# Two Q/K buffers instead of three, and one more weight tile loaded beside attention

## The chip, the cores and the metric

The kernel runs on one core of a Trainium2 chip. The metric is device time in microseconds (us) of one execution; lower is better. The kernel before took 382.33 us (median of 3 runs, 381.64 to 383.32).

## The reference

A batch of 8 sequences of 448 tokens goes through 12 heads of attention with a sigmoid in place of the softmax. Its output, 3584 rows of 768, goes through a "soft" mixture of 8 experts: each expert sees 4 slots, a slot is a weighted mean over all rows, and every row takes back a weighted mean of the 32 slot results.

```python
# attention, per head: q, k, v are (448, 64)
scores = q @ k.T / sqrt(64) - log(448)
attn_out = sigmoid(scores) @ v
# mixture of experts on x (3584 x 768), phi (768 x 32)
logits = x @ phi
d = softmax of logits over the rows            # which rows go into a slot
slot_input = d.T @ x                           # 32 x 768
slot_out[e] = relu(slot_input[e] @ w1[e]) @ w2[e]   # w1[e] 768x1024, w2[e] 1024x768
c = softmax of logits over the slots
out = c @ slot_out                             # 3584 x 768
```

All is float32. The weights w1 and w2 are 25.2 MB each, 50.3 MB together: they are more than the core's on-chip memory holds, and they can be used only when the slot inputs are known, so after the attention of all 8 batches.

## The kernel before

**Attention.** The 96 heads are worked in 48 pairs. One Q/K tile (`qk`, 128 partitions x 896 floats, 3584 bytes a partition) holds the transposed Q and K of both heads of a pair. The 448 keys of a pair are cut into chunks of 128 with a rest of 64, and the rests of two neighbouring pairs are put together. So two pairs make seven steps: an even pair p has chunks 0, 1, 2 and a fourth step that does the rests of p and of p+1 together (so it reads both Q/K tiles), then the odd pair p+1 has chunks 0, 1, 2. There are 24 x 7 = 168 steps. Step i of the loop at L409 issues `score` (L161, TensorE: eight matmuls into PSUM, then the sigmoid on ScalarE at L165), and then `weigh` of the step two earlier (L190, TensorE: the product with V). On TensorE the two alternate, and everything else (row sums into x, transposes of x into y for the slot products, the logits and slot sums of the batch just finished) is placed between them on the other engines, or as short groups of matmuls at the batch borders (L230, L284).

**Loads.** Every DMA of the kernel is issued by SyncE (SP), in program order; an issue that has to wait holds up all that stand behind it. In the loop, step i issues, behind the `score`:

- `load_qk` (L140) where the step was the last that reads a pair's Q/K tile: the fourth step of an even pair (`u[1] == NFK`) and the last chunk of an odd pair. It fetches the pair three further on into the buffer that this step lets go, so it waits for the step's score matmuls;
- `load_unit` (L94) as often as the pace asks: a weight unit is 128 x 768 floats (3072 bytes a partition, 384 KB), 64 units make up w1 and 64 w2. `N_A` = 56 units are to be issued by step 140;

and, behind the `weigh`, `load_vl` (L152, the V rows of the rests) or `load_v` (L146), each waiting for the weigh matmuls that last read its buffer.

**On-chip memory.** The weight ring has `N_A + N_B` = 70 tiles. The first 56 (`wa`) have memory of their own. The other 14 (`wb`) are laid over the tiles of attention, in the order in which these were allocated (`first`, L112): qk0, qk1, v0, vl, att0, qk2, x0, att1, att2, v1, x1, and then y. In bytes a partition: qk and att 3584 each, v 1536, vl 512, x 5376, y 12288. A `wb` load (L465 and L466 issue all of them, behind everything that attention issues) waits until the last reader of each attention tile under it is done. From the 71st unit on a load goes into the ring's first tile again, when the expert matmuls (L472) have read it, and so on round the ring.

**After attention.** The eight experts' first products (L472, which use units 0 to 63), their second products (L579, units 64 to 127, in two halves of the columns), and the output rows (L536, L537), which SP writes in 28 stores of 384 KB (L543, L550) through ring tiles. The last units come in the second half of the second products, and 19 of the 28 stores follow the last of these products.

Of the kernel before, what the change touches and what calls it, by code (L numbers as in the profile page):

```python
# [19 lines left out]
NFK = 3  # L20
# [3 lines left out]
W_STEPS = 140  # L24
# [2 lines left out]
NFC = F // P  # L27
HALF = DM // 2
UNIT = 768
N_A = 56  # L30
N_B = 14
QW = 2 * S
NP = B * NPR
WARM = 8
# [14 lines left out]
def soft_moe_attention(ctx: ExitStack, tc: tile.TileContext, qk, v, vl, phi, w1, w2, cst, out):  # L49
# [26 lines left out]
    state = {"next": 0, "ring": 0, "wpb": None}  # L76
    utile = {}

    def ring_tile(dt=F32):
        n = state["ring"]  # L80
        state["ring"] = n + 1
        n %= N_A + N_B
        if n < N_A:
            return wpa.tile([P, UNIT], dt, name=f"wa{n}")
        return state["wpb"].tile([P, UNIT], dt, name=f"wb{n - N_A}")

    def load_unit():
        n = state["next"]
        if n >= len(units):
            return  # L90
        state["next"] = n + 1
        u = units[n]
        t = ring_tile()[:]
        nc.sync.dma_start(t, w1[u[1:]] if u[0] == "w1" else w2[u[1:]])  # L94
        utile[u] = t
# [4 lines left out]
    with ExitStack() as actx:  # L100
# [8 lines left out]
        def hold(kind, n=""):  # L109
            return ap.tile(kinds[kind], F32, name=f"{kind}{n}")  # L110

        first = [("qk", 0), ("qk", 1), ("v", 0), ("vl", ""), ("att", 0), ("qk", 2), ("x", 0)]  # L112
        first += [("att", 1), ("att", 2), ("v", 1), ("x", 1)]
        held = {k: hold(*k) for k in first}
        xs = [held.pop(("x", t)) for t in range(2)]
# [3 lines left out]
        def get(*k):  # L119
            return held.pop(k, None) or hold(*k)  # L120
# [15 lines left out]

        def load_qk(p):
            if p < NP:
                t = get("qk", p % 3)
                nc.sync.dma_start(t[:], qk[p])  # L140
                qkts[p] = t

        def load_v(p):
            if p < NP:
                t = get("v", p % 2)
                nc.sync.dma_start(t[:], v[p])  # L146
                vts[p] = t

        def load_vl(r):
            if 2 * r < NP:  # L150
                t = get("vl", "")
                nc.sync.dma_start(t[:], vl[r])  # L152
                vls[r] = t

        def score(u):
            p, c = u
            sc = ps_sc.tile([P, 2, 512], F32, name="sc")
            for t in range(2):
                pt, k0 = (p, c * P + t * 64) if c < NFK else (p + t, NFK * P)
                for h, r in enumerate(heads):  # L160
                    nc.tensor.matmul(  # L161
                        sc[64 * t:64 * t + 64, h, 0:S], qkts[pt][r, S + k0:S + k0 + 64], qkts[pt][r, 0:S],
                        start=True, stop=True)
            att = get("att", seq.index(u) % 3)
            nc.scalar.activation(att[:], sc[:, :, 0:S], AF.Sigmoid, bias=nbias[:], scale=QSCALE)  # L165
            atts[u] = att

        def weigh(u):
            p, c = u
            att = atts.pop(u)  # L170
            if c == 0 and p % 2 == 0:
                avs[p] = [ps_av.tile([P, 512], F32, name=f"av0{t}") for t in range(2)]
            if c == NFK:
                avs[p + 1] = [ps_av.tile([P, 512], F32, name=f"av1{t}") for t in range(2)]
            if p == NP - 1:
                for h, r in enumerate(heads):
                    nc.tensor.matmul(  # L177
                        avs[p][1][r, 0:S], vts[p][:, c, r], att[:, h, :], start=False, stop=(c == NFK - 1))
                return
            for t in range(2):  # L180
                row = slice(64 * t, 64 * t + 64)
                for h, r in enumerate(heads):
                    if c < NFK:
                        o, w = avs[p], vts[p][row, c, r]
                        start = c == 0 and (p % 2 == 0 or t == 0)
                        stop = c == NFK - 1 and (p % 2 == 1 or t == 1)
                    else:
                        o, w = avs[p + t], vls[p // 2][row, r]
                        start, stop = t == 1, t == 0
                    nc.tensor.matmul(o[t][r, 0:S], w, att[row, h, :], start=start, stop=stop)  # L190

        def evac_a(p):
            nc.scalar.copy(x_of(p), avs[p][1][:, 0:S])  # L193

        def evac_b(p):
            av = avs.pop(p)
            nc.vector.tensor_tensor(out=x_of(p), in0=x_of(p), in1=av[0][:, 0:S], op=ALU.add)  # L197
# [20 lines left out]
        def turn_pe(px, p):  # L218
            for c in range(NBK):
                n = P if c < NBK - 1 else 64  # L220
                nc.tensor.transpose(out=px[0:n, c * P:(c + 1) * P], in_=x_of(p)[:, c * P:c * P + n], identity=ident)
# [5 lines left out]
        def logits(lg, b, pairs, js=(3, 2, 1, 0)):  # L227
            for hp in pairs:
                for j in js:
                    nc.tensor.matmul(  # L230
                        lg[32 * j:32 * j + 32, 0:BLK * nblk(j)], phi_sb[:, hp, :],
                        blocks(x_of(b * NPR + hp), j, nblk(j)),
                        start=(hp == 0), stop=(hp == NPR - 1))
# [84 lines left out]
        def last_job(b, lgt, pw, px):  # L318
# [45 lines left out]
            return sT, finish  # L364

        load_qk(0)
        load_v(0)
        load_qk(1)
        load_vl(0)
        load_v(1)  # L370
        nc.sync.dma_start(phi_sb, phi)
        nc.sync.dma_start(csb[:], cst)
        load_qk(2)
        pw = ps_av.tile([P, 512], F32, name="av00")
        for _ in range(WARM):
            nc.tensor.matmul(pw[:, 0:WN], acc[:, 0:P], acc[:, 0:WN], start=True, stop=True)  # L376
# [4 lines left out]
        for r in range(NP // 2):  # L381
            p = 2 * r
# [3 lines left out]
        for b in range(B):  # L386
            u = b * per_b + LAG
# [4 lines left out]
        for b in range(B - 1):  # L392
            u = (b + 1) * per_b + LAG
# [9 lines left out]
        def work(n):  # L403
            while todo and n > 0:
                k, turn = todo.popleft()
                turn()
                n -= k

        for i in range(len(seq) + LAG):  # L409
            for f in early.get(i, ()):  # L410
                f()
            if i < len(seq):
                u = seq[i]
                score(u)
                if u[1] == NFK:
                    load_qk(u[0] + 3)
                elif u[0] % 2 == 1 and u[1] == NFK - 1:
                    load_qk(u[0] + 3)
                while state["next"] < min(N_A, (i + 1) * N_A // W_STEPS):
                    load_unit()  # L420
            if i == len(seq) - 1:
                lgt = ps_sc.tile([P, 2, 512], F32, name="sc")
                nc.vector.memset(lgt[64:128, 0, 96:128], NEG)
            if i == len(seq):
                dmx = small.tile([1, 1], F32, name="dmx")
                nc.scalar.activation(dmx[:], atts[seq[-1]][0:1, 0, 0:1], AF.Exp)
                logits(lgt[:, 0, :], B - 1, range(NPR - 1))
            for f in middle.get(i, ()):
                f()
            if i >= LAG:  # L430
                u = seq[i - LAG]
                weigh(u)
                p, c = u
                if c == NFK:
                    evac_b(p)
                    load_vl(p // 2 + 1)
                elif c == NFK - 1:
                    load_v(p + 2)
                    if p == NP - 1:
                        work(B * S)  # L440
                        pw = ps_av.tile([P, 512], F32, name="av00")
                        px = [ps_av.tile([P, 512], F32, name="av01")]
                        px += [ps_sc.tile([P, 2, 512], F32, name="sc")[:, 0, :], ps_av.tile([P, 512], F32, name="av10")]
                        turn_pe(px[0], p - 1)
                        continue
                    evac_a(p)
                    if p % 2 == 1:
                        evac_b(p)
            for f in late.get(i, ()):
                f()  # L450
            work(rate.get(i, PACE))
# [12 lines left out]

    for _ in range(N_B):  # L465
        load_unit()  # L466
# [184 lines left out]
```

## Time and profile before

| | |
|---|---|
| median of 3 runs | 382.33 us |
| the profiled execution | 382.41 us, of which the span from first to last instruction is 380.6 us |
| TensorE matmul busy | 357.8 us (94%) |
| VectorE / ScalarE busy | 252.7 us (66%) / 224.3 us (59%) |
| moved by DMA | 95.26 MB, mean 250 GB/s |
| weight units | 112 into `wa` tiles, 16 into `wb` tiles, 384 KB each |
| Q/K loads | 48 of 448 KB, median 3.5 us from issue to landing |

Busy shares are over the whole span, which here has two stretches with different limits; the page's rows of 40 slices (9.5 us each) show where one ends and the other begins. In the timeline a group of instructions has its start, its length and its count; "SPq" is SyncE's queue, whose rows are the issues of DMAs. "Landing" is the time from such an issue to the DMA's completion.

### The profile page before, as it was taken

Reading aid. Unit: us, or ns where it says so; the run is one execution under the profiler, and the core shown is the slowest. Engines: PE = TensorE matmul, PEld = TensorE weight load, DVE = VectorE, ACT = ScalarE, POOL = GpSimd, SP = SyncE. Lnnn points to the kernel's source line nnn. Section 1 sums busy time; section 2 is a strip of 40 time slices with the busy share of each in tenths; the row PEclk is TensorE's granted clock in tenths of the full one; section 3 lists DMA queues with packets and bytes.
Section 4 is the critical chain, followed back from the end, with each engine's and each line's share of the span. In section 5 each row is a group of like instructions: output and inputs, shape, how many; then the busy total and the mean of one; then the engine's idle time right before and its main releaser. Section 6 shows DMA issues by size and latency. Waiting matters only on the chain.

```text
span 380.6 us, 10176 instructions
## 1 busy us (share of the span) xinstructions
PE 357.8 (94%) x4132; PEld 158.4 (42%) x4132; DVE 252.7 (66%) x681; ACT 224.3 (59%) x310; POOL 4.9 (1%) x23
## 2 busy tenths in 40 slices
PE   8999999999999999999999999999999969989750
PEld 5444444444444444444444444444446533422430
DVE  0148868886889688788968896886846762132560
ACT  4777766766768677667767676776761213422450
POOL 0000000000000000000000000000000000100000
PEclk9999999999999999999999999999999987999895
DMA  7677575766656675757667575534369999999998
GB/s 258 212 252 255 165 257 176 254 217 189 219 190 216 235 241 197 236 180 246 213 186 250 169 236 203 146 102 134 91 219 388 397 397 400 397 400 395 396 399 301
DMA packets 42382, 95.26 MB, mean 250 GB/s; under 512 B 4448, under 2 KB 18528, under 8 KB 42336
## 3 DMA queue, kind: packets, MB, share of 16 engines
q1 hardware_dynamic: 42336, 94.62, 72.0%
q8 instruction: 32, 0.52, 0.5%
q14 instruction: 14, 0.11, 0.1%
HBM read 83.59 MB, written 11.01 MB: 249 GB/s over the span
## 4 chain that ended last, share of the span: by engine, by line
PE 83%; DVE 7%; DMA 3%; ACT 2%; issue 1%; DVEq 0%; ACTq 0%
PE sc L161 34%; PE av L190 33%; PE po L579 5%; PE sc L230 3%; PE sc L284 3%; DMA wb<-in_w_dram 2%; PE pt L517 2%; PE av L376 1%; PE ph L536 1%; DVE tmp L486 1%; DMA out_dram<-wa 1%; DVE tmp L485 1%; DVE wa L537 1%; PE pt L536 1%; PE av L177 1%
## 5 line engine op out<-in xcount | busy, mean ns | idle before, releaser
L165 ACT ACTIVATE att<-sc,nbias 128x896 f32<-128x896 f32 x168 | 169.2, 1008 | 85.2 <-PE sc L161 82.1
L161 PE MATMUL sc<-qk 64*64 64x448 f32 x1344 | 157.2, 538 | 0.4 <-ACT att L165 0.4
L212 DVE STREAM_TRANSPOSE y<-x 32x384 f32<-32x384 f32 (+5 forms) x352 | 143.4, 407 | 5.7
L190 PE MATMUL av<-att,v 64*64 64x448 f32 x1128 | 131.4, 536 | 0.0
L161 PEld LDWEIGHTS sc<-qk 64*64 64x64 f32 x1344 | 49.8, 133 | 72.6 <-issue 60.8
L190 PEld LDWEIGHTS av<-att,v 64*64 64x64 f32 x1128 | 43.1, 133 | 62.8 <-issue 61.3
L197 DVE TENSOR_TENSOR x<-x,av 128x448 f32<-128x448 f32 x47 | 29.2, 621 | 41.4 <-PE av L190 29.7
L579 PE MATMUL po<-wa,hw 128*32 128x384 f32 x224 | 24.8, 513 | 0.3 <-DMA wa<-in_w_dram 0.3
L193 ACT COPY x<-av 128x448 f32<-128x448 f32 x47 | 24.6, 523 | 0.0
L190 PE MATMUL av<-att,vl 64*64 64x448 f32 x192 | 22.4, 536 | 0.0
L472 PE MATMUL ph<-wa,phit 128*32 128x256 f32 x336 | 18.5, 379 | 0.0
L472 PEld LDWEIGHTS ph<-wa,phit 128*32 128x32 f32 x336 | 10.7, 110 | 6.9
L536 PE MATMUL ph<-lt,wb 128*128 128x384 f32 x28 | 12.7, 453 | 1.0 <-DVE lt L566 1.0
L537 DVE COPY wa<-pt 128x384 f32<-128x384 f32 x21 | 10.9, 554 | 2.9 <-PE pt L536 2.6
L537 ACT COPY wa<-ph 128x384 f32<-128x384 f32 x21 | 9.8, 480 | 4.9 <-PE ph L536 4.2
L230 PE MATMUL sc<-x,phit 128*32 128x96 f32 (+1 forms) x384 | 12.3, 262 | 0.3 <-DVE x L202 0.3
L230 PEld LDWEIGHTS sc<-x,phit 128*32 128x32 f32 x384 | 9.9, 110 | 6.2 <-ACT x L193 4.9
L536 PE MATMUL pt<-lt,wb 128*128 128x384 f32 x28 | 10.4, 373 | 1.6 <-DVE lt L566 1.6
L190 PEld LDWEIGHTS av<-att,vl 64*64 64x64 f32 x192 | 7.3, 133 | 10.7 <-issue 10.7
L306 DVE SCALAR_TENSOR_TENSOR acc<-acc,t,sc 128x192 f32<-128x192 f32 x6 | 2.5, 413 | 13.5 <-PE sc L284 13.5
L488 ACT COPY t<-tmp 128x32 f32<-128x32 f32 x8 | 1.7, 218 | 15.8 <-DVE tmp L486 15.8
L507 DVE CAST tmp<-lt 128x128 fp32r<-128x128 f32 x8 | 1.8, 227 | 13.7 <-PE pt L517 13.4
(106 smaller groups left out, 178.6 us busy)
## 6 DMA issues: line engine op xcount, KB each, us to landing
wa<-in_w_dram SPq DMA_DIRECT2D x112, 384.0 KB, 6.2
qk<-in_qk_dram SPq DMA_DIRECT2D x48, 448.0 KB, 3.5
v<-in_v_dram SPq DMA_DIRECT2D x48, 192.0 KB, 2.6
out_dram<-wa SPq DMA_DIRECT2D x21, 384.0 KB, 5.2
wb<-in_w_dram SPq DMA_DIRECT2D x16, 384.0 KB, 6.1
out_dram<-wb SPq DMA_DIRECT2D x7, 384.0 KB, 7.7
vl<-in_vl_dram SPq DMA_DIRECT2D x24, 64.0 KB, 2.6
csb<-in_cst_dram SPq DMA_DIRECT2D x1, 128.0 KB, 4.6
```

The lines of the kernel that those rows point to most:

```text
L161: nc.tensor.matmul(sc[64 * t:64 * t + 64, h, 0:S], qkts[pt][r, S + k0:S + k0 + 64], qkts[pt][r, 0:S], start=True, stop=True)
L165: nc.scalar.activation(att[:], sc[:, :, 0:S], AF.Sigmoid, bias=nbias[:], scale=QSCALE)
L190: nc.tensor.matmul(o[t][r, 0:S], w, att[row, h, :], start=start, stop=stop)
L193: nc.scalar.copy(x_of(p), avs[p][1][:, 0:S])
L197: nc.vector.tensor_tensor(out=x_of(p), in0=x_of(p), in1=av[0][:, 0:S], op=ALU.add)
L212: nc.vector.transpose(ys[t][32 * g:32 * g + 32, a, k0:k0 + n, 0:nblk(g), :], src)
L230: nc.tensor.matmul(lg[32 * j:32 * j + 32, 0:BLK * nblk(j)], phi_sb[:, hp, :], blocks(x_of(b * NPR + hp), j, nblk(j)), start=(hp == 0), sto ...
L284: nc.tensor.matmul(sl[32 * a:32 * a + 32, 0:SLN], zt[:, c * BLK:(c + 1) * BLK], yt[:, :, a, :, c, :], start=(c == 0), stop=(c == NBK - 1))
L472: nc.tensor.matmul(ph[32 * j:32 * j + 32, 0:256], sT[:, kc, :], utile[("w1", e, j, kc // 3)][:, kc % 3 * 256:(kc % 3 + 1) * 256], start=(k ...
L536: nc.tensor.matmul(pf[:, 0:HALF], ct_of(m), st, start=True, stop=True)
L537: (nc.scalar.copy, nc.vector.tensor_copy)[n % 2](ov, pf[:, 0:HALF])
L579: nc.tensor.matmul(po[32 * fl:32 * fl + 32, 0:HALF], h[:, k:k + NSLOT], ut, start=(n == 0), stop=(n == 2 * E - 1))
```

## The change

The change has four parts: two Q/K buffers where there were three, so that a pair's Q/K is fetched when the pair two before it has been scored (not three before), and one Q/K load less ahead of the loop; a ring of 57 tiles of its own and 13 laid over attention's (again 70); another order of allocation of the attention tiles; and weight units that are issued only in the steps that issue a Q/K load, right behind it, as many as the pace asks for by then.

```diff
-N_A = 56
-N_B = 14
+N_A = 57
+N_B = 13
@@ the order of the attention tiles
-        first = [("qk", 0), ("qk", 1), ("v", 0), ("vl", ""), ("att", 0), ("qk", 2), ("x", 0)]
+        first = [("qk", 0), ("v", 0), ("vl", ""), ("att", 0), ("qk", 1), ("x", 0)]
         first += [("att", 1), ("att", 2), ("v", 1), ("x", 1)]
@@ load_qk
-                t = get("qk", p % 3)
+                t = get("qk", p % 2)
@@ ahead of the loop
         nc.sync.dma_start(csb[:], cst)
-        load_qk(2)
@@ in the loop, behind the score of step i
-                if u[1] == NFK:
-                    load_qk(u[0] + 3)
-                elif u[0] % 2 == 1 and u[1] == NFK - 1:
-                    load_qk(u[0] + 3)
-                while state["next"] < min(N_A, (i + 1) * N_A // W_STEPS):
-                    load_unit()
+                if u[1] == (NFK - 1 if u[0] % 2 else NFK):
+                    load_qk(u[0] + 2)
+                    while state["next"] < min(N_A, (i + 1) * N_A // W_STEPS):
+                        load_unit()
```

## The prediction

> **What bounds the kernel now.** I read the page's slices first, since shares over the whole span hide the two stretches.
>
> ```profile
> span 380.6 us, 10176 instructions
> PE   8999999999999999999999999999999969989750
> DMA  7677575766656675757667575534369999999998
> ```
>
> TensorE (PE) is full for some 29 slices, up to about 280 us, and the DMA engines are not; then DMA is full to the end while TensorE has holes. The table of stretches shows the same in numbers (time, busy time of the five engines, granted clock, DMA share, GB/s):
>
> ```profile
> 20.00:240.00 220.00, 220.00 (x2620) 93.62 (x2616) 176.29 (x461) 153.25 (x184) 0.00 (x0) 1.00 0.66 215
> 240.00:272.00 32.00, 32.00 (x392) 13.76 (x388) 25.57 (x71) 21.92 (x28) 0.00 (x0) 1.00 0.37 110
> 272.00:277.50 5.50, 5.50 (x67) 2.16 (x59) 4.93 (x10) 4.37 (x7) 0.00 (x0) 1.00 0.60 179
> 277.50:278.50 1.00, 1.00 (x14) 0.29 (x8) 0.73 (x3) 0.55 (x1) 0.00 (x0) 1.00 0.00 0
> 278.50:281.00 2.50, 2.50 (x48) 1.36 (x48) 0.04 (x1) 2.43 (x3) 0.00 (x0) 1.00 0.68 216
> 281.00:286.00 5.00, 4.24 (x50) 2.66 (x50) 2.40 (x11) 2.53 (x10) 0.00 (x0) 1.00 0.95 313
> 286.00:345.00 59.00, 54.84 (x726) 25.95 (x714) 28.38 (x97) 15.72 (x45) 3.78 (x17) 0.94 1.03 396
> 345.00:374.00 29.00, 19.17 (x85) 9.16 (x84) 12.57 (x24) 11.22 (x24) 0.21 (x1) 0.87 1.03 395
> ```
>
> So attention is TensorE's: 252 us of 252 busy from 20 to 272 us at the full granted clock. Whatever gives it no work less makes it no shorter, and whatever lets it wait makes it longer one for one. From about 281 us the end belongs to DMA: 396 GB/s at a share of 1.03, without a pause. One weight unit is 384 KB, and in the 40 us from 300 to 340 the transfer view counts
>
> ```profile
> wa<-in_w_dram SPq DMA_DIRECT2D x41, 384.0 KB, 7.8
> ```
>
> 41 units, so 40 / 41 = **0.98 us a unit** (393,216 bytes at 396 GB/s are 0.99). Does the end hang on this stream? The chain of waits says so:
>
> ```profile
> 343.84 0.78 PE po L579 x8
> 344.62 0.14 PE ph L536
> 344.76 7.87 DMA wb<-in_w_dram
> 352.68 0.86 PE po L579 x4
> ```
>
> The last product of the experts starts when the last unit lands (344.76 + 7.87 = 352.63), and DMA stays full behind it to 374 us with the stores. A unit more or less behind attention is therefore 0.98 us at the end, as long as DMA does not run dry.
>
> **Part 1: the 57th tile of its own.** It looks like one unit out of the full stretch: attention has DMA time to spare (share 0.37 from 240 to 272 us), so 71 units would be left, where 72 were, and the end 0.98 us earlier. That is right only if the units that lie over attention's tiles come as early as before. Here are the first four of them, then what each waited for, then the matmuls that let them go:
>
> ```profile
> 272.09 0.43 SPq L94 DMA_DIRECT2D wb<-in_w_dram  x1
> 273.94 0.33 SPq L94 DMA_DIRECT2D wb<-in_w_dram  x1
> 277.75 0.33 SPq L94 DMA_DIRECT2D wb<-in_w_dram  x1
> 279.41 0.33 SPq L94 DMA_DIRECT2D wb<-in_w_dram  x1
> ```
> ```profile
> SPq L94 <- PE sc L161: 1.4, 1, 1.4
> SPq L94 <- PE av L190: 3.4, 1, 3.4
> SPq L94 <- PE av L177: 1.3, 1, 1.3
> ```
> ```profile
> 272.98 0.93 PE L161 MATMUL sc<-qk 64*64 64x448 f32 x8
> 276.73 0.93 PE L190 MATMUL av<-att,vl 64*64 64x448 f32 x8
> 278.35 0.97 PE L177 MATMUL av<-att,v 128*64 128x448 f32 x4
> ```
>
> They are the 57th to 60th unit. With 3072 bytes a tile over the attention tiles in their order, the layout before is: 57th over qk0 (free since pair 45 was scored, so it goes at once behind the last V load); 58th over qk0 and qk1 (pair 46, whose last score ends at 273.9: the wait of 1.4); 59th over qk1, v0 and vl (the weigh at 276.73, over at 277.7: the wait of 3.4); 60th over att0 (the weigh at 278.35: the wait of 1.3). All three waits agree with the bytes, so I trust the same sum for the new order, qk0, v0, vl, att0, qk1, x0, att1, att2, v1, x1, y:
>
> - 57th: has its own tile, moved in attention;
> - 58th: bytes 0 to 3072, qk0 alone. Pair 46 now lies there, so again about 273.94;
> - 59th: bytes 3072 to 6144: qk0, v0, vl (ends at 5632) and 512 bytes of att0. So it waits for the weigh at 278.35 and goes at **279.41, not 277.75**;
> - 60th: att0, free at the same time, so right behind it, at the place that the 61st had;
> - 61st: qk1 and x0, and so on: all further ones queue in order, and the tiles over x1 and y begin with the same unit as before (66th and 68th: 57 x 3072 less 3584 bytes is 512 less than 56 x 3072).
>
> So the early unit is gone again. Before, 59 units had been issued when the weigh of 278.35 let the 60th go; now 58 have. The one that moved into attention frees a place at 272.09, where nothing hurried, and SP then stands until 279.41 with DMA idle (in the stretch 277.5 to 278.5 it was idle already). From there unit n + 1 stands where unit n + 2 stood: everything behind is one place, 0.98 us, later.
>
> Can the stretch from 278.5 to 286 swallow a unit? It moved 216 and 313 GB/s where 396 go, (396 - 216) x 2.5 + (396 - 313) x 5 = 865 KB less than it could, over two units. So the term's lower end is 0. But that room was there while several units were queued, and the new kernel issues no more of them earlier. At that stretch's own 313 GB/s a unit takes 393 / 313 = 1.26 us, the upper end. I take **+0.98 us**, the pace of the full stretch, since every place behind moves at it. The Trainium skill ("DMA: Bandwidth & Descriptors", section "Specifications") gives about 358 GB/s as the limit of HBM for one core; by it the unit would cost an estimated 1.10 us. The trace moves 396 here, so the trace's price stands.
>
> **Part 2: two Q/K buffers.** The trigger of a Q/K load doesn't move (the same score lets a buffer go); its use comes one pair earlier. Before, a load had seven or eight steps; now it must land within four steps. The trace has one case where this would just fail:
>
> ```profile
> 63.43 0.43 SPq L94 DMA_DIRECT2D wa<-in_w_dram  x1
> 65.28 0.33 SPq L140 DMA_DIRECT2D qk<-in_qk_dram  x1
> DMA to landing us min/median/max: 4.7/4.7/4.7
> 69.95 0.15 PEld L161 LDWEIGHTS sc<-qk 64*64 64x64 f32 x4 [0.22 <-issue]
> ```
>
> Issue at 65.28, and the next pair's first weights of the score at 69.95: **4.67 us of time**, against a landing of 4.7. For a load of an odd pair it is 0.37 us more: its rests come in the second half of a step's score, and the rows at 272.98 and 276.73 are five groups of eight matmuls apart, 0.75 us each, 1.5 us a step. Where logits or slot matmuls fall between, it is more by their time. All 45 loads of the loop landed within
>
> ```profile
> DMA to landing us min/median/max: 3.1/3.5/4.9
> ```
>
> so the median has 1.2 us to spare. The long one above had a weight unit issued 1.85 us ahead of it, in the same queue. That is what the fourth part takes away: units now go only behind a Q/K load, so the nearest unit ahead is one issued with the load before, three or four steps (4.5 or 6 us) earlier. What is new is two units at a time (17 of the 40 loads with units have two). The trace has that too:
>
> ```profile
> 221.06 0.33 SPq L140 DMA_DIRECT2D qk<-in_qk_dram  x1
> 221.44 0.90 SPq L94 DMA_DIRECT2D wa<-in_w_dram  x2
> 227.04 0.33 SPq L140 DMA_DIRECT2D qk<-in_qk_dram  x1
> DMA to landing us min/median/max: 3.2/3.2/3.2
> ```
>
> The landing is that of the load at 221.06: two units close behind it don't hold it up. Lower end of this term: 0, as TensorE has no idle time there to give back. Upper end: 23 loads of even pairs, each landing at the longest 4.9, so 23 x 0.23 = 5.3 us. I take **0**: with no unit close ahead, the loads are nearest to the median row. The added wait at SP stands ahead of V loads, which have two pairs' time.
>
> **Part 3: the start and the moved units.** One Q/K load and one unit fewer are issued ahead of the fourth step; the first three pairs' use isn't near. V, rests and their order are unchanged; the pace still ends in step 140, with DMA at 0.37 behind it. 0 us, hidden by TensorE's full stretch; without that cover it would be one Q/K transfer, some 1.2 us at the pace above.
>
> **Sum.** 382.41 (the profiled execution) + 0.98 + 0 + 0 = 383.39. The median shown is 0.08 lower than that execution, so **383.3 us**, 0.3% more than before.
>
> **The rivals.**
>
> A. *The unit is won after all.* If the 59th does not wait for att0 (the layout's bytes fall otherwise than I count), 71 units stand where 72 did: 382.33 - 0.98 = 381.4 us. For it: DMA is full from 286 us on. Against it: three waits that fit my bytes. Chance 0.12.
>
> B. *The late unit is swallowed* in the room of 865 KB between 278.5 and 286: 382.3 us. Against it: the issues from 279.41 on follow one another with nothing to pull forward. Chance 0.14.
>
> C. *Slower: Q/K lands late.* The place is the first score of an even pair; the mechanism that a load lies in the queue behind a burst of two units and the V loads; it decides from a landing above 4.67 us. If half of the 23 even pairs' loads land at 4.9, TensorE stands 12 x 0.23 = 2.8 us, and with the 0.98 the time is 386.1; if all do, 388.6. For it: one row of 4.7 and a longest of 4.9. Against it: those had a unit close ahead, and the new order leaves none. The Trainium skill ("DMA: Bandwidth & Descriptors", section "Latency and other measured facts") has HBM's access latency go from 0.2 us to 2 us at high load; put on the shortest landing, that would be an estimated 4.9 us for a load under full traffic. Chance 0.12.
>
> **How the numbers follow.** The forecast has 0.62, with 382.6 to 384.2 as its own range (the term's ends of 0 and 1.26, and the runs' spread). A measurement of this kernel can tell about 0.5%, 1.9 us, so 380.4 to 384.2 counts as the same: the forecast, A and B lie in it whole, but for 0.03 of A (a low run, a margin I don't see), and C lies above it with 0.10 of its 0.12. Faster 0.03, same 0.87, slower 0.10. The range takes in A at its middle and the near end of C: 381.3 to 385.2.
>
> **What would show it.** In the new profile: the unit issued at about 273.9 as the first over attention's tiles, the next at about 279.4 with a wait for the L177 weigh, DMA share 0 in some microseconds before it; from 286 us on 396 GB/s as before, and landings one unit later; the span 381.6. Q/K landings with a longest under 4.7, and the first score after the seventh step never waiting for a DMA; TensorE full from 20 to 272 us. I am wrong on part 1 if the second unit over attention's tiles is issued before 279 us, or if attention's end moves; on part 2 if the waits list scores (L161) that waited for the Q/K DMA with more than 0.5 us in all.

## The result, and the profile after

The changed kernel took 384.16 us (median of 17 runs, 383.58 to 386.88) against 382.42 us of the kernel before (17 runs, 381.22 to 383.44): a ratio of 1.0059, 95% interval 1.0045 to 1.0072. The medians differ by 1.74 us, 0.45%, which is less than the ratio says; five of the 17 runs took over 385 us. A second series, beside three of the experiments, gave 384.40 us against 382.64, ratio 1.0040 (1.0027 to 1.0054), a difference of 1.76 us between the medians. The profiled execution took 383.65 us, near the low end of the first series.

The page's slices, which answer to those of before:

```profile
span 381.9 us, 10181 instructions
PE   8999999999999999999999999999999969989740
DMA  4677575765657765847766576434359999999998
```

and the table of stretches (time, busy time of the five engines, granted clock, DMA share, GB/s):

```profile
20.00:240.00 220.00, 220.00 (x2614) 94.75 (x2608) 175.92 (x460) 152.66 (x184) 0.00 (x0) 1.00 0.67 219
240.00:272.00 32.00, 32.00 (x392) 13.75 (x388) 25.57 (x71) 21.93 (x27) 0.00 (x0) 1.00 0.42 124
274.00:279.50 5.50, 5.50 (x56) 1.88 (x48) 4.12 (x11) 4.01 (x5) 0.00 (x0) 1.00 0.24 74
279.50:281.50 2.00, 2.00 (x46) 1.37 (x46) 0.00 (x0) 1.93 (x3) 0.00 (x0) 1.00 0.29 74
286.00:346.00 60.00, 55.83 (x734) 26.38 (x734) 29.16 (x100) 16.60 (x47) 3.79 (x17) 0.97 1.03 397
346.00:375.00 29.00, 18.39 (x82) 8.00 (x80) 11.69 (x23) 10.14 (x23) 0.21 (x1) 0.90 1.04 398
```

The two stretches with their two limits are the same, and so is the pace of the second (397 GB/s). New is the quiet ahead of it: from 274 to 281.5 us DMA moves 74 GB/s. Here is why, in SP's issues of the first units over attention's tiles, the waits ahead of the second, and the matmuls that let it go:

```profile
274.33 0.33 SPq L94 DMA_DIRECT2D wb<-in_w_dram  x1
279.81 0.33 SPq L94 DMA_DIRECT2D wb<-in_w_dram  x1
280.18 1.40 SPq L94 DMA_DIRECT2D wb<-in_w_dram  x1
```
```profile
SPq L94 <- PE av L177: 5.0, 1, 5.0
```
```profile
277.88 0.93 PE L161 MATMUL sc<-qk 64*64 64x448 f32 x8
278.74 0.97 PE L177 MATMUL av<-att,v 128*64 128x448 f32 x4
```

The 58th unit goes behind the score of pair 46, the 59th waits 5.0 us for the weigh at 278.74, as the bytes said. The chain's end then hangs on the last unit (346.05 + 7.80 = 353.85, where it was 352.63), as before:

```profile
338.11 7.88 DMA wa<-in_w_dram
346.05 7.80 DMA wb<-in_w_dram
353.90 0.86 PE po L576 x4
```

What the forecast had put at 0 is in attention. The issues around 20 to 28 us, the landing of the Q/K load at 24.20, and the weight load of the score that waits for it:

```profile
19.66 0.33 SPq L140 DMA_DIRECT2D qk<-in_qk_dram  x1
20.04 0.90 SPq L94 DMA_DIRECT2D wa<-in_w_dram  x2
21.95 0.33 SPq L146 DMA_DIRECT2D v<-in_v_dram  x1
23.48 0.33 SPq L152 DMA_DIRECT2D vl<-in_vl_dram  x1
24.20 0.33 SPq L140 DMA_DIRECT2D qk<-in_qk_dram  x1
```
```profile
DMA to landing us min/median/max: 5.6/5.6/5.6
```
```profile
29.89 0.13 PEld L161 LDWEIGHTS sc<-qk 64*64 64x64 f32 x1 [0.53 <-DMA qk<-in_qk_dram]
```

A burst of two units, V and the rests' V stood ahead of it; it took 5.6 us where 5.0 were to be had. The span can be put together from three places: how much later than before the eighth step's score starts, what is lost between that and the last step's score, and from the start of that last score to the end. Read off the timelines in this way (for the changed kernel the last score's row, at 277.88, stands above, and the span is 381.87: 381.87 - 277.88 = 103.99; for the kernel before the row is the one below, and 380.64 - 277.49 = 103.15), the profiled executions give, in us:

```profile
277.49 0.93 PE L161 MATMUL sc<-qk 64*64 64x448 f32 x8
```

| kernel | start | lost in attention | last score to end | span |
|---|---|---|---|---|
| before | 0 | 0 | 103.15 | 380.64 |
| before, another execution | +0.68 | 0 | 102.49 | 380.66 |
| changed | -0.31 | 0.71 | 103.99 | 381.87 |
| changed, another execution | +0.54 | 0.78 | 104.24 | 383.04 |

The start is not the change's: two executions of the same kernel differ by 0.7 there. The other two columns are. The busy time doesn't show the late load: from 20 to 240 us TensorE stands at 220.00 of 220.00 us in both kernels, since some matmul was in flight at every moment while half of a score waited. The list of waits and the start of a later step show it.

### The profile page after: what moved, and what is told of

Its sections match the earlier page's. It is cut to its first block, busy times and chain, and to the rows that moved or that the text cites. A ratio compares the mean times of both kernels' runs of the same rounds, so it can differ in the third digit from the quotient of the medians.

```text
span 381.9 us, 10181 instructions
## 1 busy us (share of the span) xinstructions
PE 358.0 (94%) x4132; PEld 158.5 (42%) x4132; DVE 252.4 (66%) x681; ACT 223.7 (59%) x310; POOL 4.9 (1%) x23
## 4 chain that ended last, share of the span: by engine, by line
PE 80%; DMA 13%; DVE 1%; ACT 1%; issue 1%; DVEq 0%; SPq 0%; ACTq 0%
PE sc L161 34%; PE av L190 32%; DMA wa<-in_w_dram 10%; PE ph L469 5%; PE sc L230 3%; PE sc L284 3%; DMA wb<-in_w_dram 2%; DMA out_dram<-wa 1%; PE av L375 1%; PE av L177 1%; DVE wa L534 0%; PE av L291 0%; PE ph L533 0%; PE pt L533 0%; ACT att L165 0%
## 5 line engine op out<-in xcount | busy, mean ns | idle before, releaser
L161 PE MATMUL sc<-qk 64*64 64x448 f32 x1344 | 161.3, 539 | 0.4 <-ACT att L165 0.4
L190 PE MATMUL av<-att,v 64*64 64x448 f32 x1128 | 135.1, 536 | 0.0
L161 PEld LDWEIGHTS sc<-qk 64*64 64x64 f32 x1344 | 51.7, 133 | 73.0 <-issue 60.3
L190 PEld LDWEIGHTS av<-att,v 64*64 64x64 f32 x1128 | 44.8, 133 | 61.9 <-issue 60.4
L576 PE MATMUL po<-wa,hw 128*32 128x384 f32 x228 | 27.5, 511 | 0.4 <-DMA wa<-in_w_dram 0.2
L469 PE MATMUL ph<-wa,phit 128*32 128x256 f32 x342 | 19.8, 379 | 0.0
L533 PE MATMUL ph<-lt,wb 128*128 128x384 f32 x28 | 11.8, 420 | 1.1 <-DVE lt L563 1.0
L576 PEld LDWEIGHTS po<-wa,hw 128*32 128x32 f32 x228 | 6.5, 111 | 12.3 <-issue 5.5
L533 PE MATMUL pt<-lt,wb 128*128 128x384 f32 x28 | 9.5, 341 | 1.6 <-DVE lt L563 1.6
```

The source lines that it names most:

```text
L161: nc.tensor.matmul(sc[64 * t:64 * t + 64, h, 0:S], qkts[pt][r, S + k0:S + k0 + 64], qkts[pt][r, 0:S], start=True, stop=True)
L469: nc.tensor.matmul(ph[32 * j:32 * j + 32, 0:256], sT[:, kc, :], utile[("w1", e, j, kc // 3)][:, kc % 3 * 256:(kc % 3 + 1) * 256], start=(k ...
L533: nc.tensor.matmul(pf[:, 0:HALF], ct_of(m), st, start=True, stop=True)
L576: nc.tensor.matmul(po[32 * fl:32 * fl + 32, 0:HALF], h[:, k:k + NSLOT], ut, start=(n == 0), stop=(n == 2 * E - 1))
```

## The experiments

Ratios are to the kernel before on the same chip; tables give the profiled execution in the columns above.

**One place in the DMA stream.** First with three Q/K buffers, so that the tail stands alone. One unit late (e1):

```diff
-        first = [("qk", 0), ("qk", 1), ("v", 0), ("vl", ""), ("att", 0), ("qk", 2), ("x", 0)]
+        first = [("qk", 0), ("qk", 1), ("att", 0), ("v", 0), ("vl", ""), ("qk", 2), ("x", 0)]
```

> The kernel before (three Q/K buffers, units at every step, 14 tiles over attention) with one thing changed: att0 is allocated ahead of v0 and vl, so that the 59th unit lies over att0 and waits for the weigh at 278 us, as in the changed kernel. Theory 'one place later': the 59th is issued at about 279.4 instead of 277.75, everything behind lands one place later, +0.8 to +1.0 us (about 383.3), attention unchanged, the runs as close together as those of before. Rival 'the late unit is swallowed': within 0.3 us of before. Rival 'all of the loss is Q/K landing late': 0, since Q/K has three buffers here.

Measured: 383.88 us, ratio 1.0034 (1.0019 to 1.0049), so 0.7 to 1.9 us; the 59th went at 279.47. The profiled execution was the series' fastest (382.52 us; last score to end 103.20, no more than before), the others lay from 382.96 to 384.76. In the series the late unit costs about what was expected; that one execution lost nothing by it, so a part can be swallowed at times.

Three units late (e9):

```diff
+        first = [("att", 0), ("qk", 0), ("qk", 1), ("v", 0), ("vl", ""), ("qk", 2), ("x", 0)]
```

> The kernel before with att0 allocated first, so that the 57th unit already waits for the weigh at 278.35 and the 58th and 59th stand behind it in the queue: three units late instead of the one of the changed kernel. Theory 'one place later, 0.98 us each': +2.9 us at the end, 385.3. Rival 'the stretch from 279 to 286 swallows a unit or two': +1 to +2, 383.5 to 384.5. Rival 'the tail isn't set by this stream': 0.

Measured: 385.92 us (385.87 to 386.09, 4 runs), ratio 1.0082 (1.0060 to 1.0103), so 3.1 us, 1.05 a place; last score to end 106.21, three above before. SP's issues and the wait ahead of them:

```profile
279.99 1.70 SPq L94 DMA_DIRECT2D wb<-in_w_dram  x2
```
```profile
SPq L94 <- PE av L177: 7.3, 1, 7.3
```

The unit's price holds, and the stretch to 286 us does not swallow a place as a rule.

The other way, the 60th unit earlier with three buffers (e4):

```diff
+        first = [("qk", 0), ("qk", 1), ("v", 0), ("vl", ""), ("qk", 2), ("att", 0), ("x", 0)]
```

> The kernel before with qk2 allocated ahead of att0: the 60th unit then waits for the last score (278.4) and not for the weigh that ends at 279.4. Theory 'places': the DMA's idle or half idle stretch around 280 to 281 us is closed, the full stretch starts up to one unit earlier: 0.5 to 1.0 us faster than before, 381.4 to 381.9. Rival 'the stretch from 279 to 286 swallows such shifts': no change.

Measured: 383.23 us, ratio 1.0015 (1.0001 to 1.0029); last score to end 103.38. Not faster (if anything 0.15% slower, which its profile doesn't explain), so my expectation fell. The likely reason, argued and not shown: by then only the 59th was ahead, and getting the next out a microsecond sooner fills a room that is there anyway. A unit that is not yet issued when the stream starts costs; one issued sooner than needed won nothing here.

**Two buffers with the 59th cured.** The changed kernel, qk1 ahead of att0 (e2):

```diff
-        first = [("qk", 0), ("v", 0), ("vl", ""), ("att", 0), ("qk", 1), ("x", 0)]
+        first = [("qk", 0), ("v", 0), ("vl", ""), ("qk", 1), ("att", 0), ("x", 0)]
```

> The changed kernel with qk1 allocated ahead of att0: the 59th and 60th unit then lie over v0, vl and qk1 and wait only for the last score (ends about 278.4) and not for the weigh of the step before last (279.4). Theory 'one place later plus late Q/K': the tail wins back up to 0.98 us against the changed kernel, 383.3 or so, and the runs stay as wide apart as the changed kernel's (some 1.5 to 3 us above their lowest), because Q/K is as late as there. Rival 'it is all the tail': 382.4 with runs as close as before's. Rival 'it is all late Q/K': no better than the changed kernel, 384.2.

Measured: 383.32 us, ratio 1.0017 (1.0002 to 1.0031), so below the changed kernel's (clear of its first series' interval, overlapping its second's). Last score to end 102.67, and in attention 0.88 lost, all of it at the same load as in the changed kernel: the sixth pair's, which took 5.8 us here. The runs lie within 1.8 us. Neither single cause explains it: the tail is won, the stall stays.

**Q/K late behind a burst.** The cure alone: at most one unit ahead of the near load, two ahead of the far one (e3).

```diff
-                    while state["next"] < min(N_A, (i + 1) * N_A // W_STEPS):
+                    for _ in range(min(N_A - state["next"], 2 if u[0] % 2 else 1)):
                         load_unit()
```

> The changed kernel with another spread of the units behind the Q/K loads: one behind the load at an even pair's fourth step (the next load follows three steps later) and two behind the load at an odd pair's last chunk (the next follows four steps later), instead of two at most of the first and one at most of the second. Theory 'a Q/K load is late behind a burst of two units': landings of the loads of odd pairs fall to 4 us and less, no score waits for a DMA, and the time is before + 0.98 - 0.3 for the shorter start, 383.0 to 383.4, with runs close together (within 2 us). Rival 'it is all the tail' or 'the landings are late by something else': as the changed kernel, 384.2 with runs up to 387.

Measured: 383.69 us (383.28 to 384.54), ratio 1.0034 (1.0021 to 1.0047): the runs lie within 1.3 us, the changed kernel's within 3.3 and 2.0. In attention nothing is lost (one weight load waits 0.2 us, which delays nothing), and last score to end is 104.29. So what is left is the tail's place, the same 0.34% as with three buffers; the medians differ by 0.99 us.

The cause made larger: three units behind each even pair's load, none behind the others (e5).

```diff
-                    while state["next"] < min(N_A, (i + 1) * N_A // W_STEPS):
+                    while u[0] % 2 == 0 and state["next"] < min(N_A, (i + 5) * N_A // W_STEPS):
                         load_unit()
```

> The changed kernel with all weight units behind the loads at the even pairs' fourth step: bursts of three (mostly), none behind the others. The next Q/K load, of an odd pair, follows three steps later. Theory 'a Q/K load is late behind a burst': a third unit of 0.98 us ahead of it moves landings of odd pairs' loads from a usual 3.5 to 4.8 us up to 4.5 to 5.8; against 5.0 us of time a good half of the loads without logits or slot work between come late, by some 0.3 to 0.8 us: TensorE stands 2 to 8 us in all, the time is 386 to 392. Rival 'landings don't depend on the burst, the one late load is late by chance': as the changed kernel, 384.2.

Measured: 387.76 us (386.26 to 388.05), ratio 1.0122 (1.0099 to 1.0145). The waits of that profile (total, times, longest):

```profile
PEld sc L161 <- DMA qk<-in_qk_dram: 2.4, 4, 1.5
PE sc L161 <- DMA qk<-in_qk_dram: 0.7, 1, 0.7
```

The second line is no place of its own: it is TensorE itself, idle at the longest of the four waits.

```profile
159.44 0.14 PEld L161 LDWEIGHTS sc<-qk 64*64 64x64 f32 x2 [1.51 <-DMA qk<-in_qk_dram]
159.44 0.59 PE L161 MATMUL sc<-qk 64*64 64x448 f32 x2 [0.73 <-DMA qk<-in_qk_dram]
```

So four loads, all of odd pairs, are waited for where the changed kernel has one; 3.03 us are lost in attention, and last score to end is 103.96. The late loads follow the size of the burst. They were fewer than expected (four, not half of the odd pairs'): ten landed after 4.8 us or more, but five of these stood near a batch's border, where the matmuls of the logits come between a load and its use and give 1.6 us more. Three waits are of 0.3 us, the low end of what I expected, and one is of 1.5.

The other way to undo the bursts, units at every step as before, with two buffers (e6):

```diff
                 if u[1] == (NFK - 1 if u[0] % 2 else NFK):
                     load_qk(u[0] + 2)
-                    while state["next"] < min(N_A, (i + 1) * N_A // W_STEPS):
-                        load_unit()
+                while state["next"] < min(N_A, (i + 1) * N_A // W_STEPS):
+                    load_unit()
```

> The changed kernel with units again issued at any step, as before: two buffers, no bursts, but a unit can stand 1.5 to 1.9 us ahead of a Q/K load. Theory: some loads land in 4.7 to 5.2 us as the kernel before shows (4.7 against 4.67 us of time), so several small stalls of 0.1 to 0.7 us instead of one, in all 0.5 to 2 us: 384 to 385.5. Rival 'only bursts of two make loads late': no stall, 383.3 to 383.6, better than the changed kernel.

Measured: 384.09 us, ratio 1.0025 (1.0015 to 1.0035); nothing lost in attention, last score to end 103.83. My expectation of several small stalls fell and its rival held: no score waits, and what is left is about one place of the tail (the medians differ by 0.87 us). Some luck is in it: one load of an odd pair took 5.5 us here, but near a batch's border, where it has 1.6 us more. With two buffers the late load comes with the fourth part of the change, the units in bursts behind the loads.

That order with three buffers, so that a late load harms nothing (e7):

```diff
                 if u[1] == (NFK - 1 if u[0] % 2 else NFK):
-                    load_qk(u[0] + 2)
+                    load_qk(u[0] + 3)
```

(in the kernel before, 56 and 14 tiles)

> The kernel before with the issue order of the changed one alone: weight units only behind a Q/K load, three Q/K buffers, 56 and 14 tiles. Theory of two terms: with three buffers a load that lands in 5 or 6 us is in time and the tail is that of before, so no change: 382.3 to 383.0, within 0.15%. Rival 'the bursts cost DMA time by themselves': +0.25% or more, as the changed kernel has over its tail term.

Measured: 383.29 against 383.22 us, ratio 0.9998 (0.9989 to 1.0007). The longest of its landings is as long as in the changed kernel, and behind the same burst (issued at 25.1 us),

```profile
DMA to landing us min/median/max: 2.9/3.4/5.6
```

and no score waits. So the bursts cost nothing in DMA time; they cost only by being ahead of a load with 5.0 us of time.

**Both cures.** The changed kernel with the two edits of e2 and e3 (e8):

```diff
+        first = [("qk", 0), ("v", 0), ("vl", ""), ("qk", 1), ("att", 0), ("x", 0)]
+                    for _ in range(min(N_A - state["next"], 2 if u[0] % 2 else 1)):
```

> The changed kernel with both cures: one unit behind the even step's load and two behind the odd one's, and qk1 allocated ahead of att0. Theory of two terms (a place in the DMA stream, and Q/K landing late behind a burst): both are gone but for a small rest (the 59th still goes at about 278.4 and not 277.75), so 382.3 to 383.0, within 0.15% of before, and no score waits for a DMA. Rival 'two Q/K buffers cost something else as well': 383.3 or more, as each cure alone.

Measured: 383.29 us (382.22 to 385.60), ratio 1.0020 (1.0004 to 1.0036), above what I expected and at the edge of its rival, that two buffers cost something else as well. Last score to end 103.17; 0.26 lost in attention at one load that took 5.2 us with no unit issued in the 5 us ahead of it, late in the loop. An instruction transfer fell into that load's time (more on these at the end), so a burst is not the only thing that makes a load late. With the layout made exact, 512 unused bytes behind vl, so that the 59th ends on them (e10, which is e8 with this tile, set to zero once):

```diff
+        first = [("qk", 0), ("v", 0), ("vl", ""), ("pad", ""), ("qk", 1), ("att", 0), ("x", 0)]
```

> Two buffers, one unit behind the even step's load and two behind the odd one's, and the layout qk0, v0, vl, 512 unused bytes, qk1, att0: the 59th unit now ends on the unused bytes and waits for the weigh that ends at 277.7 as in the kernel before; the 60th lies over qk1 (278.4). Theory: both terms are gone, 382.2 to 382.8, no different from before (and no better: 59 units have been issued by 278 us in both). Rival 'two buffers win a unit when the layout lets them': 381.4.

Measured: 382.88 us against 383.22, ratio 1.0001 (0.9992 to 1.0011). Its issues and its landings:

```profile
274.36 0.33 SPq L94 DMA_DIRECT2D wb<-in_w_dram  x1
278.23 0.33 SPq L94 DMA_DIRECT2D wb<-in_w_dram  x1
278.91 0.33 SPq L94 DMA_DIRECT2D wb<-in_w_dram  x1
```
```profile
DMA to landing us min/median/max: 2.9/3.4/4.6
```

With 57 tiles, two buffers and both causes taken away the loss is gone to within 0.1%, and nothing is won, as 59 units are out by then in either kernel. No version beat the kernel before.

**Two more executions.** The kernels before and after once more, for their profiles (the table above):

> The kernel before once more, for a profile of another execution. Theory: no score waits for a DMA, the last score starts 262.4 to 263.0 us after the eighth step's, and the time from the last score's start to the end of the span is again 103 us give or take 0.3, against 104.0 and 104.2 in the two profiles of the changed kernel. Rival 'the tail of one execution is chance': 104 or more.

> The changed kernel once more, on the chip of the other three, with a profile of another execution. Theory: the load of the sixth pair (index 5, behind a burst of two and an instruction fetch) is late again at about 30 us by some 0.7 us, and the first units over attention's tiles go at about 274 and 280; 384.0 to 384.6. Rival 'late by chance': no score waits, or at another place.

Before (382.43 us): no score waited, last score to end 102.49, somewhat under the margin expected. After: the same load late (5.7 us) and the wait for it

```profile
30.82 0.14 PEld L161 LDWEIGHTS sc<-qk 64*64 64x64 f32 x2 [0.60 <-DMA qk<-in_qk_dram]
```

so it is no chance of one execution: the same load, in all three profiles with this issue order and two buffers (the changed kernel twice, and with qk1 ahead of att0).

## Why the prediction was right or wrong

**The time** is within the range (384.16 in 381.3 to 385.2) but 0.9 above the forecast. Whether it is still "the same", where I had put 0.87, hangs on the measure: the ratio of 0.59% is over the 0.5% that I allowed, the median lies just inside the 384.2, and the second series, 0.40%, is under it. The likeliest case alone, +0.98 from the tail and nothing else, was not what happened: it was that together with the mechanism of rival C, at one load where C had counted twelve. That the time still came so near is luck in part. The two terms, 0.98 and 0.71 to 0.78, make 1.7 to 1.8 us, and the medians of the two series differ by 1.74 and 1.76.

**Part 1 was right, in mechanism and in size.** The layout by bytes gave the 59th's wait, shown in the waits. (One slip that nothing hangs on: the 61st unit lies over qk1 alone, and x0 begins under the 62nd.) Last score to end, averaged over the profiles with 59 units out before the weigh of 278 us (the two of before, e4, e7 and e10: 103.15, 102.49, 103.38, 102.95, 102.71) is 102.94; over those with 58 (the two of the changed kernel, e1, e3, e5, e6: 103.99, 104.24, 103.20, 104.29, 103.96, 103.83) 103.92; with 56 106.21. The place forecast at 0.98 measures 0.98 so, and in the runs of e1 and e3, which have nothing else, 1.3 us (0.7 to 1.9). Single profiles of one group lie up to 1.1 apart. In e2 and e8 the 59th goes 1.0 us after the last score's start, not 1.9 as in the changed kernel, and they lie with the first group (102.67 and 103.17). Rival A, the unit won, is refuted; B, swallowed, holds for single executions (e1's) but not as a rule.

**Part 2 failed at one step**: "I take 0: with no unit close ahead, the loads are nearest to the median row". I had looked at how close the nearest unit stands, and for the bursts at the load ahead of the two units, not at the next load behind them. That next load, an odd pair's, follows three steps later, and by then two units, V and the rests' V stand in the same queue. The row that I took for proof was the wrong one. The profile before has a right one, a load with two units, V and the rests' V issued in the 5 us ahead of it:

```profile
147.34 0.42 SPq L94 DMA_DIRECT2D wa<-in_w_dram  x1
149.25 0.33 SPq L146 DMA_DIRECT2D v<-in_v_dram  x1
149.63 0.42 SPq L94 DMA_DIRECT2D wa<-in_w_dram  x1
150.78 0.33 SPq L152 DMA_DIRECT2D vl<-in_vl_dram  x1
151.50 0.33 SPq L140 DMA_DIRECT2D qk<-in_qk_dram  x1
DMA to landing us min/median/max: 4.8/4.8/4.8
```

The upper end was too low as well: the longest landing of 4.9 us came from one execution; the other execution of the kernel before has 5.2, and e1 and e9, with the same three buffers and issue order, 5.8. The runs showed 0.71 and 0.78 us lost at one load in the two profiles. Over the series the medians give the same, 1.74 and 1.76 us less e3's 0.99; the ratios, less e3's 0.34%, give 0.25% (1 us) by the first series and 0.06% by the second, so the size is rough. The single executions between 385 and 387 us were not profiled; that they have more such loads is likely by e5, not shown. Of the signs that I had set, the waits of scores for Q/K told of it (0.53 and 0.60 us, where I had said 0.5); TensorE full from 20 to 272 us could not, as it stayed full.

**Rival C's point was right, its place half so.** It decides at the time to the next use; but the even pairs' loads, with 4.67 us, had no loss. It was the odd pairs', with 5.0, since theirs is the one with a burst ahead. A price of its size came only with bursts of three (e5: 4.7 us in all, the tail's place included), and from four loads, not from half of 23.

**Part 3** was right: units and Q/K at the start made no difference that shows beside what the start varies by anyway (0.7 us between the two executions of the kernel before, 0.85 between those of the changed one).

## What to carry to other kernels

When tiles of a later stage lie over those of an earlier one, lay out the bytes and write down which reader frees each tile: a tile of its own more is worth nothing if the next one then ends 512 bytes inside a buffer that is freed last. When a buffer is taken from a load, work out the time from its trigger to its use, and sum up all that the queue carries in the time before its issue, not only what stands right ahead; if it is near, spread the other loads so that the larger burst falls into the longer gap. Take the longest landing from several executions, not from one.

## What the runs showed of the hardware that I had not expected

**Instruction transfers share the queue's engines.** In the transfer view of the 3 us from 23 to 26 us of the changed kernel

```profile
q1 hardware_dynamic: 523, 0.92, 91.5%
q8 instruction: 1, 0.02, 1.9%
```

one instruction packet took 1.9% of 16 engines, 0.9 us of one of them. In each of the three profiles with the late load one such packet falls into its window. The fourteen profiles together show what it is worth: they hold 638 Q/K loads issued after 9 us. By the number of weight units issued in the 5 us ahead of a load, and by whether an instruction packet was moving in the first 2.8 us of it, the mean time to landing is, in us (number of loads):

| units ahead | no packet | a packet |
|---|---|---|
| 0 | 3.29 (264) | 3.67 (90) |
| 1 | 3.50 (145) | 3.78 (72) |
| 2 | 4.20 (28) | 4.75 (27) |
| 3 | 5.11 (7) | 5.32 (5) |

So the burst weighs most, and a packet goes with 0.2 to 0.6 us more. Of the loads behind two units 9 of 27 with a packet took over 5.0 us, and 3 of 28 without. The late load of the changed kernel had both against it. That a packet delays a load by keeping one engine from its rows is argued; no run here moved such a packet.

**The start varies by the matmuls' own pace.** The first two scores took, in the kernel before and in its other execution,

```profile
4.83 1.73 PE L161 MATMUL sc<-qk 64*64 64x448 f32 x16
```
```profile
4.83 2.41 PE L161 MATMUL sc<-qk 64*64 64x448 f32 x16
```

0.68 us apart with the same start. The Trainium skill ("TensorE: Matmul & The Clock Gate", section "Part 1: The HAM clock gate (the "warmup" mystery)") says that the number of slow first matmuls varies from run to run with the phase of the window that raises the clock; these two rows agree with it. The granted clock reads 1.00 from 4 to 7 us in both executions, so it doesn't show the difference.
